# Second MLP product of a token-mixing block: five wide products per step, an order of work written by hand, low halves added to the output by transfers

## The chip, the core and the metric

The kernel runs on one core of a Trainium2 chip. The core has a matrix engine (PE, whose weight loads are listed as PEld), a vector engine (DVE), an activation engine (ACT), a general engine (POOL) and a queue engine (SP) that mostly issues transfers. They run side by side, each through its own list of instructions in order, and wait for each other by semaphores. Matrix results go to PSUM, eight banks of 2 KB per partition; everything else lies in SBUF, 128 partitions wide. Transfers between the chip's memory and SBUF run on 16 DMA engines that all queues share.

The metric is device time in microseconds (us), median over runs.

## The reference

A sequence of S = 2048 tokens of D = 512 channels goes through a linear-attention block and then through a mixer MLP, both with a residual:

```python
h  = x + _A_ref(_layernorm(x), wqkv, w_phi, wo)
# mixer: the MLP acts across the tokens, shared over the channels
hn = _layernorm(h)
u  = gelu(einsum("bsd,sf->bdf", hn, w1) + b1)      # F = 1792
y  = einsum("bdf,fs->bds", u, w2) + b2
out = h + y.transpose(0, 2, 1)
```

All data is float32, and the result must be accurate to float32's order, so a product of two matrices is made of three: each operand is split into a high part that the matrix engine takes exactly (`F32R`) and a low part (the rest), and high x high, high x low and low x high are added up.

## The kernel before, in words

The core first does the attention part, then the first MLP product (`w1`, tiles `pu`, function `fill`, helper `mm3`), then the second (`w2`, tiles `py`). The change is in the second, and in how its first weights come in while the first is still running.

**Winograd form.** The second product multiplies `w2` blocks of 2 x 2 (two blocks of 128 rows of F, two blocks of 128 output tokens) with `u` blocks of 2 x 2 (the same two blocks of F, two halves of 256 channels, `HD`). Instead of eight block products it forms seven, from sums and differences of the four blocks on each side (Strassen's scheme in Winograd's form). The `u` side, `operands_u`, makes seven operands for each pair of F blocks once and keeps their high and low parts in SBUF (`UB[p, m]`, p from 0 to 6); for p below 2 they lie in the tiles `un`, for the others in `uf`, and the last of them are made while the second product starts.

**Steps.** `STEPS` runs over 8 super-steps `sp` (two output tiles of 128 tokens each) and within each over 7 pairs `p` of F blocks: 56 steps. Each step does seven products, each of three matmuls of 128 x 128 weights and 256 columns (`product`, line 789), so 1176 matmuls. The weights are the `w2` parts, the columns the `u` parts. A super-step collects its seven products in four banks, half a bank (256 columns) for each sum that is needed; p = 0 opens them, p = 6 closes them. Odd super-steps use the banks of the pools `ps_f` and `ps_q`, even ones those of `ps_b`.

**Weights.** `stream_w2` works on groups of two steps (`GRP`): two transfers of 256 KB issued by SP (line 773, 1 KB pieces), four operations on DVE that form the sums (lines 777 to 780), ACT's copy into the high parts `whi` (line 57) and DVE's subtraction for the low parts `wlo` (line 58), 1792 elements per partition each. The raw tiles have three buffers, `whi` and `wlo` two.

**Emptying the banks.** After p = 6 the seven sums are combined: ACT copies half a bank (line 820), DVE does three additions (821 to 823) and two operations of 512 elements that add the bias `b2` (825). The two finished tiles are then added to `out`, which already holds `h`, by accumulating transfers that POOL issues (line 827). The last super-step reads `h` back into `hb` instead, adds there, and writes the sums with plain transfers (lines 830 to 847).

**Order.** Except where the code fixes it, a scheduler decides the order of each engine's instructions from a timeline of its own. In the second product it may mix the steps' matmuls, and it spreads the sums of later groups between the operations that empty banks. `issue_after(LO[-18])` keeps the first sums of `w2` behind a given low part of `w1`. SP issues the first three groups' loads of `w2` early in the first product.

The lines that matter most:

```python
def product(o, a, b, start, stop):
    for i, (x, y) in enumerate(((0, 0), (0, 1), (1, 0))):
        nc.tensor.matmul(o, a[x], b[:, y], start=start and i == 0, stop=stop and i == 2, skip_group_check=True)
```

Of the kernel before, what the change touches and what calls it, by code (L numbers as in the profile page):

```python
# [21 lines left out]
NF = F // P  # L22
NG = 8
NPR = 2 * NG
# [9 lines left out]
def block_kernel(ctx: ExitStack, tc: tile.TileContext, x, xT, wT, phic, wo, w1, b1, w2, b2,  # L34
# [20 lines left out]
    def split(hi, lo, src, lo_engine):  # L55

        nc.scalar.activation(hi, src, AF.Copy)  # L57
        lo_engine.tensor_sub(lo, src, hi)  # L58
# [535 lines left out]
    w1v = w1.rearrange("(k p) f -> p k f", p=P)  # L594
    w2v = w2.rearrange("(k p) s -> p k s", p=P)

# [7 lines left out]
    def stream(src, k0, n, c0, w):  # L604

        raw = wf.tile([P, n, w], F32, name="wraw")
        wh_ = wf.tile([P, n, w], F32R, name="whi")
        wl_ = wf.tile([P, n, w], F32R, name="wlo")
        nc.sync.dma_start(raw, src[:, k0:k0 + n, c0:c0 + w])
        nc.scalar.activation(wh_, raw, AF.Copy)  # L610
        LATER.append((wl_, raw, wh_))
        return wh_, wl_

    PU, WI, LO = {}, {}, []
    FN, FL = [0] * (NF // 2), [0] * (NF // 2)
# [93 lines left out]

    NP = NF // 2  # L710
    HD = D // 2
    up = ctx.enter_context(tc.tile_pool(name="up", bufs=1, side="right", reuse_waits="tile"))
# [50 lines left out]
    STEPS = [(sp, p) for sp in range(NT // 2) for p in range(NP)]  # L763
    GRP = 2
    AW = {}

    def stream_w2(n):
        steps = STEPS[n:n + GRP]
        raw = ws.tile([P, GRP, 7, P], F32, name="wraw", bufs=3)
        wh_ = ws.tile([P, GRP, 7, P], F32R, name="whi")  # L770
        wl_ = ws.tile([P, GRP, 7, P], F32R, name="wlo")
        for i, (sp, p) in enumerate(steps):
            nc.sync.dma_start(raw[:, i, 0:4].rearrange("p (k i) s -> p k (i s)", k=2),
                              w2v[:, 2 * p:2 * p + 2, sp * 2 * P:(sp + 1) * 2 * P])
            AW[sp, p] = wh_[:, i], wl_[:, i]
        with tc.issue_after(LO[-18]):
            nc.vector.tensor_add(raw[:, :, 4], raw[:, :, 0], raw[:, :, 2])
            nc.vector.tensor_sub(raw[:, :, 0], raw[:, :, 1], raw[:, :, 0])
            nc.vector.tensor_sub(raw[:, :, 5], raw[:, :, 4], raw[:, :, 1])
            nc.vector.tensor_sub(raw[:, :, 6], raw[:, :, 3], raw[:, :, 5])  # L780
        split(wh_, wl_, raw, nc.vector)


    PROD = ((1, 1, 0, 0, True), (2, 6, 2, 1, True), (3, 3, 3, 1, True), (4, 4, 2, 0, False), (0, 0, 1, 0, True),
            (5, 5, 0, 1, False), (6, 2, 3, 0, False))

    def product(o, a, b, start, stop):
        for i, (x, y) in enumerate(((0, 0), (0, 1), (1, 0))):
            nc.tensor.matmul(o, a[x], b[:, y], start=start and i == 0, stop=stop and i == 2, skip_group_check=True)  # L789

    def products(sp, ps, order):
        for a, b, bk, half, opens in order:
            for p in ps:
                wh_, wl_ = AW[sp, p]
                product(bank[bk][:, half], (wh_[:, a], wl_[:, a]), UB[p, b], p == 0 and opens, p == NP - 1)

    def flat(a):
        return a.rearrange("p k d -> p (k d)")

    for n, (sp, p) in enumerate(STEPS):  # L800
        t = 2 * sp
        last = t + 2 == NT
        if n % GRP == 0:
            stream_w2(n)
        if p == 0:
            pools = [ps_f, ps_f, ps_q, ps_q] if sp % 2 else [ps_b] * 4
            bank = [pool.tile([P, 2, HD], F32, name="py", tag="pu") for pool in pools]
        if p < NP - 1 - last:
            products(sp, [p], PROD)
            continue  # L810
        if p < NP - 1:
            continue
        by_bank = sorted(PROD, key=lambda m: m[2:4])
        e = uo.tile([P, 2, HD], F32, name="e")
        u2 = uo.tile([P, HD], F32, name="u2", bufs=1)
        u3 = uo.tile([P, HD], F32, name="u3")
        if not last:
            products(sp, [p], by_bank)
            ot = uo.tile([P, 2, 2, HD], F32, name="ot", bufs=1)
            nc.scalar.activation(e[:, 1], bank[0][:, 0], AF.Copy)  # L820
            nc.vector.tensor_add(u2, bank[0][:, 1], e[:, 1])
            nc.vector.tensor_add(u3, bank[1][:, 0], u2)
            nc.vector.tensor_add(e[:, 0], bank[2][:, 0], u2)
            for i, add in enumerate((u3.unsqueeze(1).to_broadcast([P, 2, HD]), e)):
                nc.vector.scalar_tensor_tensor(ot[:, i], bank[2 + i], b2s[:, t + i:t + i + 1], add,  # L825
                                               op0=ALU.add, op1=ALU.add)
                nc.gpsimd.dma_start(out[(t + i) * P:(t + i + 1) * P, :], flat(ot[:, i]), accum_op=ALU.add)  # L827
# [6 lines left out]
        products(sp, [p - 1, p], by_bank)  # L834
        nc.scalar.activation(e[:, 1], bank[0][:, 0], AF.Copy)
        nc.vector.tensor_add(hb[1][:, 1], bank[0][:, 0], hb[1][:, 1])
        nc.vector.tensor_add(u2, bank[0][:, 1], e[:, 1])
        nc.vector.tensor_add(hb[1][:, 0], u2, hb[1][:, 0])
        nc.vector.tensor_add(u3, bank[1][:, 0], u2)
        nc.vector.tensor_add(hb[0], hb[0], u3.unsqueeze(1).to_broadcast([P, 2, HD]))  # L840
        nc.vector.tensor_add(hb[0][:, 0], bank[2][:, 0], hb[0][:, 0])
        nc.vector.tensor_add(hb[1][:, 0], bank[2][:, 0], hb[1][:, 0])
        nc.vector.tensor_add(hb[0][:, 1], bank[2][:, 1], hb[0][:, 1])
        nc.sync.dma_start(out[t * P:(t + 1) * P, :], flat(hb[0]))
        for k, q in ((0, nc.scalar), (1, nc.sync)):
            nc.vector.tensor_add(hb[1][:, k], bank[3][:, k], hb[1][:, k])
            q.dma_start(out[(t + 1) * P:NT * P, k * HD:(k + 1) * HD], hb[1][:, k])


def _layout(A_x, A_wqkv, A_w_phi, A_wo, B_w1, B_b1, B_w2, B_b2):  # L850
# [7 lines left out]
    for a in range(P // DH):  # L858
        for c in range(2):
            f = (2 * c + a % 2) * DH  # L860
            mask[a * DH:(a + 1) * DH, f:f + DH] = 1.0

    wo = np.asarray(A_wo).reshape(2, 4, 2, 32, D).transpose(2, 0, 1, 3, 4).reshape(D, D)
    return {
# [6 lines left out]
        "b1": np.asarray(B_b1).reshape(NF, P).T,  # L871
        "w2": np.asarray(B_w2),
        "b2": np.asarray(B_b2).reshape(NT, P).T,
# [21 lines left out]
```

## Time and profile before

| | |
|---|---|
| median of 3 runs | 535.17 us |
| lowest and highest run | 534.43 and 535.64 us |
| span of the profiled execution, first to last instruction | 532.6 us |
| the profiled execution's own time | not recorded beside its span; the timed runs' median is 2.57 us above the span |
| PE busy | 520.8 us, 98% of the span |
| weight loads (PEld) | 448.7 us, 84% |
| DVE, ACT, POOL busy | 384.4, 271.9, 234.8 us |
| second product on PE (`py`) | 385.8 to 527.1 us |
| its matmuls | 1176, listed as 283 ns each |
| accumulating transfers | 14 of 256 KB, median 4.8 us to landing |
| loads of `w2` in 400 to 520 us | 44 of 256 KB, median 3.2 us to landing |

A matmul is listed with its full duration, but matmuls overlap: the next one starts before the last one has drained. What one costs is therefore read from start to start, not from its mean duration. The same holds, to a smaller degree, for DVE and ACT. "Idle before, releaser" names what ended an engine's waiting. The time from issue to landing of a transfer is from the queue engine's issue to the signal that the data is there.

### The profile page before, as it was taken

The page shows a single profiled execution, that of the slowest core. Times are in us where ns is not written, and L with a number is a line of the kernel's source. Part 1 is how long each engine was busy: PE and PEld are TensorE (multiplying, and loading weights), DVE is VectorE, ACT ScalarE, POOL GpSimd, SP SyncE. Part 2 cuts the span into 40 slices and gives each one's busy share as a digit, 9 for nine tenths or more (in the row PEclk, how much of TensorE's full clock was granted, in tenths as well). Part 3 has the DMA queues.
Part 4 walks back from the last instruction along what each step waited for, and adds up shares of the span by engine and source line. Part 5 has one row for each costly group of instructions (what it writes and reads, how often), then busy time and mean ns, then how long its engine had stood idle before and what let it go on. Part 6 is the DMA issues. An engine that isn't in the chain of part 4 may idle for free.

```text
span 532.6 us, 9386 instructions
## 1 busy us (share of the span) xinstructions
PE 520.8 (98%) x3616; PEld 448.7 (84%) x3616; DVE 384.4 (72%) x680; ACT 271.9 (51%) x460; POOL 234.8 (44%) x190
## 2 busy tenths in 40 slices
PE   8999999999999989999999999999999999999995
PEld 7888888886877767777788888888899999999995
DVE  6993999877699989875325524835668877887784
ACT  6998844424336776557746423525444243343340
POOL 2589699877889988887325000000001101100110
PEclk9999999999999999999999999999999999999999
DMA  8633310020502233334255333542014556535631
GB/s 309 206 110 118 99 22 21 1 72 9 160 0 79 82 101 116 104 116 136 85 176 159 98 100 98 159 117 82 20 41 107 143 148 153 123 120 136 143 75 46
DMA packets 45486, 55.81 MB, mean 105 GB/s; under 512 B 3969, under 2 KB 33025, under 8 KB 45441
## 3 DMA queue, kind: packets, MB, share of 16 engines
q1 hardware_dynamic: 43136, 51.38, 30.7%
q0 software_dynamic: 2016, 3.67, 5.5%
q8 instruction: 28, 0.46, 0.4%
q10 hardware_dynamic: 288, 0.17, 0.1%
q14 instruction: 18, 0.14, 0.1%
HBM read 46.81 MB, written 8.39 MB: 104 GB/s over the span
## 4 chain that ended last, share of the span: by engine, by line
PE 83%; POOL 9%; DVE 3%; ACT 2%; issue 1%; DVEq 0%; POOLq 0%; ACTq 0%
PE py L789 26%; PE pu L62 11%; PE pu L63 11%; PE pu L64 11%; POOL ez L442 4%; POOL eq L460 3%; PE pv L63 2%; PE pv L64 2%; PE pv L62 2%; PE pk_ps L62 2%; PE pk_ps L63 2%; PE pk_ps L64 2%; POOL hs L58 2%; PE po L62 1%; PE kvp L207 1%; PE po L63 1%
## 5 line engine op out<-in xcount | busy, mean ns | idle before, releaser
L827 POOL DMA_DIRECT2D out<-ot x14 | 12.5, 1001 | 212.2 <-DVE ot L825 212.2
L789 PE MATMUL py<-uf,whi 128*128 128x256 f32 x560 | 96.2, 283 | 0.0
L63 PE MATMUL pu<-hs,whi 128*128 128x512 f32 x224 | 87.6, 391 | 1.8 <-POOL hs L58 1.8
L602 DVE TENSOR_TENSOR wlo<-wraw,whi 128x512 fp32r<-128x512 f32 x56 | 50.3, 903 | 51.8 <-ACT whi L610 50.7
L57 ACT ACTIVATE whi<-wraw 128x1792 fp32r<-128x1792 f32 x28 | 47.7, 1705 | 77.9 <-PE py L789 73.8
L62 PE MATMUL pu<-hs,whi 128*128 128x512 f32 x224 | 87.4, 395 | 0.0
L64 PE MATMUL pu<-hs,wlo 128*128 128x512 f32 x224 | 87.2, 390 | 0.0
L789 PEld LDWEIGHTS py<-uf,whi 128*128 128x128 f32 x560 | 83.3, 192 | 0.0
L789 PE MATMUL py<-uf,wlo 128*128 128x256 f32 x280 | 69.9, 283 | 0.0
L58 DVE TENSOR_TENSOR wlo<-wraw,whi 128x1792 fp32r<-128x1792 f32 x28 | 56.6, 2022 | 15.4 <-ACT whi L57 15.4
L610 ACT ACTIVATE whi<-wraw 128x512 fp32r<-128x512 f32 x56 | 35.0, 627 | 47.0 <-PE pu L63 44.8
L63 PEld LDWEIGHTS pu<-hs,whi 128*128 128x128 f32 x224 | 42.1, 188 | 11.0 <-POOL hs L58 2.8
L62 PEld LDWEIGHTS pu<-hs,whi 128*128 128x128 f32 x224 | 42.0, 188 | 10.9 <-issue 2.5
L64 PEld LDWEIGHTS pu<-hs,wlo 128*128 128x128 f32 x224 | 42.0, 188 | 9.1 <-DVE wlo L602 0.4
L789 PEld LDWEIGHTS py<-uf,wlo 128*128 128x128 f32 x280 | 49.7, 192 | 0.0
L442 POOL TENSOR_TENSOR ez<-eq,zB 128x1024 f32<-128x1024 f32 x16 | 40.9, 2559 | 2.5 <-ACT zB L488 2.5
L789 PE MATMUL py<-un,whi 128*128 128x256 f32 x224 | 38.4, 283 | 0.0
L195 POOL TENSOR_TENSOR pk<-pk,sk 128x1024 f32<-128x1024 f32 x16 | 31.0, 1941 | 9.8 <-DVE sk L194 9.0
L460 POOL TENSOR_TENSOR eq<-eq,w 128x1024 f32<-128x1024 f32 x16 | 32.0, 1997 | 4.0 <-DVE w L457 4.0
L789 PEld LDWEIGHTS py<-un,whi 128*128 128x128 f32 x224 | 33.2, 192 | 0.1
L199 POOL TENSOR_TENSOR zacc<-zacc,pk 128x1024 f32<-128x1024 f32 x13 | 31.3, 2405 | 0.6
L58 POOL TENSOR_TENSOR hs<-hn,hs 128x512 fp32r<-128x512 f32 x16 | 21.4, 1340 | 17.5 <-ACT hs L57 15.6
(165 smaller groups left out, 1176.5 us busy)
## 6 DMA issues: line engine op xcount, KB each, us to landing
wraw<-in_w SPq DMA_DIRECT2D x112, 256.0 KB, 2.9
xraw<-in_xT SPq DMA_DIRECT2D x16, 256.0 KB, 3.1
xh<-in_x SPq DMA_DIRECT2D x16, 256.0 KB, 2.6
h<-in_x SPq DMA_DIRECT2D x16, 256.0 KB, 2.7
out<-h SPq DMA_DIRECT2D x16, 256.0 KB, 3.0
out<-ot POOLq DMA_DIRECT2D x14, 256.0 KB, 4.8
wraw<-in_wT SPq DMA_DIRECT2D x12, 256.0 KB, 5.0
wo<-in_wo SPq DMA_DIRECT2D x4, 256.0 KB, 3.6
```

Of the source, the lines that this page charges most:

```text
L57: nc.scalar.activation(hi, src, AF.Copy)
L58: lo_engine.tensor_sub(lo, src, hi)
L62: nc.tensor.matmul(o, ah, bh, start=first, stop=False)
L63: nc.tensor.matmul(o, ah, bl, start=False, stop=False)
L64: nc.tensor.matmul(o, al, bh, start=False, stop=last)
L195: nc.gpsimd.tensor_mul(heads(PK[t]), heads(PK[t]), sk.unsqueeze(2).to_broadcast([P, 2 * H, DH]))
L199: nc.gpsimd.tensor_add(zacc, zacc, PK[t])
L442: nc.gpsimd.tensor_mul(EZ[t], EQ[t], zB)
L460: nc.gpsimd.tensor_mul(heads(EQ[t]), heads(EQ[t]), W[t].rearrange("p g c h -> p (g c h)").unsqueeze(2).to_broadcast([P, 2 * H, DH]))
L602: LO.append(nc.vector.tensor_sub(wl_, raw, wh_).ins)
L610: nc.scalar.activation(wh_, raw, AF.Copy)
L789: nc.tensor.matmul(o, a[x], b[:, y], start=start and i == 0, stop=stop and i == 2, skip_group_check=True)
```

## The change

- The weight sums are chosen differently (another assignment of the same seven products, `PROD`), so that five of the seven products have a bank of their own. In these five, one matmul of 512 columns multiplies the high weights with the high and the low part of `u` side by side, into the two halves of the bank; one of 256 columns adds low weights x high `u` to the first half. The other two products share bank 2, half each, and stay three matmuls of 256 columns. A super-step has six banks instead of four, taken in turn from the eight.
- The last two pairs of every super-step (p = 5 and 6) are done together, bank by bank, so that banks are finished one after the other. Before, only the last super-step did so.
- In the last super-step one of the seven products (bank 5) stays narrow (`LAST`).
- The second half of banks 3, 4 and 5 now holds a contribution that must be added. ACT copies it into `low`, and POOL issues two more accumulating transfers per super-step (128 and 256 KB), four in all. In the last super-step DVE adds it.
- `w2` is laid out anew on the host, so that one transfer of 512 KB (4 KB in one piece for each partition) loads a group. Three operations on DVE form the sums instead of four. High parts have three buffers.
- `tc.manual_schedule` takes PE, DVE and ACT away from the scheduler for the second product; the order is the one in which the code stands: sums two groups ahead, low parts one group ahead. Where a group begins at p = 6, low parts stand between the operations that empty banks, and the sums behind them.
- `issue_after(LD[-20])` also keeps the first `w2` loads behind a given load of `w1`.
- The scratch memory for POOL's transfers is set to 8192.

```diff
+    def load_w2(g):
+        RAW[g] = ws.tile([P, 7, GRP * P], F32, name="wraw", bufs=3)
+        nc.sync.dma_start(RAW[g][:, 1:5], w2[g])
+    def sums_w2():
...
+        load_w2(g)
+        raw = RAW[g]
+        WH[g] = ws.tile([P, 7, GRP * P], F32R, name="whi", bufs=3)
+        nc.vector.tensor_add(raw[:, 0:2], raw[:, 1].unsqueeze(1).to_broadcast([P, 2, GRP * P]), raw[:, 2:4])
+        nc.vector.tensor_add(raw[:, 5], raw[:, 1], raw[:, 2])
+        nc.vector.tensor_add(raw[:, 6], raw[:, 4], raw[:, 5])
+        nc.scalar.activation(WH[g], raw, AF.Copy)
+    def lo_w2():
...
+        wl_ = ws.tile([P, 7, GRP * P], F32R, name="wlo", bufs=2)
+        nc.vector.tensor_sub(wl_, RAW[g], WH[g])
...
+    with tc.issue_after(LO[-18]), tc.issue_after(LD[-20]):
+        sums_w2()
+        lo_w2()
+        sums_w2()
+    PROD = ((2, 1, 0, None), (5, 5, 1, None), (0, 0, 2, 0), (1, 4, 2, 1), (3, 6, 3, None), (6, 2, 4, None),
+            (4, 3, 5, None))
+    LAST = PROD[:-1] + ((4, 3, 5, 0),)
+    def product(o, half, a, b, first, start, stop):
+        if half is None:
+            nc.tensor.matmul(o, a[0], b, start=start, stop=stop, skip_group_check=True)
+            nc.tensor.matmul(o[:, 0], a[1], b[:, 0], start=False, stop=stop, skip_group_check=True)
+            return
...
+    ctx.enter_context(tc.manual_schedule(engines={ET.PE, ET.DVE, ET.Activation}))
...
+        if n % GRP == 0 and p < NP - 1:
+            sums_w2()
+            lo_w2()
...
+        if p < NP - 2:
+            products(sp, [p], order)
             continue
         if p < NP - 1:
             continue
+        products(sp, [p - 1, p], order)
...
+            nc.scalar.activation(e[:, 1], bank[0][:, 0], AF.Copy)
+            for i in range(3):
+                nc.scalar.activation(low[:, i], bank[3 + i][:, 1], AF.Copy)
+            nc.vector.tensor_add(e[:, 1], bank[0][:, 1], e[:, 1])
+            nc.vector.tensor_sub(u2, bank[1][:, 0], e[:, 1])
+            nc.vector.tensor_add(u2, bank[1][:, 1], u2)
+            nc.vector.tensor_sub(u3, u2, bank[2][:, 0])
+            nc.vector.scalar_tensor_tensor(e[:, 0], bank[2][:, 1], -1.0, u2, op0=ALU.mult, op1=ALU.subtract)
...
+            out_block(0, 0, bank[2][:, 1], u3)
+            out_block(0, 1, bank[3][:, 0], u3)
+            nc.gpsimd.dma_start(out[t * P:(t + 1) * P, :], flat(ot[:, 0]), accum_op=ALU.add)
+            if n % GRP == 0:
+                lo_w2()
+            out_block(1, 0, bank[4][:, 0], e[:, 0])
+            out_block(1, 1, bank[5][:, 0], e[:, 1])
+            nc.gpsimd.dma_start(out[(t + 1) * P:(t + 2) * P, :], flat(ot[:, 1]), accum_op=ALU.add)
+            nc.gpsimd.dma_start(out[t * P:(t + 1) * P, HD:D], low[:, 0], accum_op=ALU.add)
+            nc.gpsimd.dma_start(out[(t + 1) * P:(t + 2) * P, :], flat(low[:, 1:3]), accum_op=ALU.add)
+            if n % GRP == 0:
+                sums_w2()
```

More of the change, by code (lines that the diff above doesn't have):

```diff
@@ L763, in block_kernel @@
     STEPS = [(sp, p) for sp in range(NT // 2) for p in range(NP)]
[L764 to L781, printed above, removed]
@@ L788, in product @@
+    LAST = PROD[:-1] + ((4, 3, 5, 0),)
[3 more added lines that the diff above has]
+            nc.tensor.matmul(o[:, 0], a[1], b[:, 0], start=False, stop=stop, skip_group_check=True)
+            return
         for i, (x, y) in enumerate(((0, 0), (0, 1), (1, 0))):
-            nc.tensor.matmul(o, a[x], b[:, y], start=start and i == 0, stop=stop and i == 2, skip_group_check=True)
+            nc.tensor.matmul(o[:, half], a[x], b[:, y], start=start and first and i == 0, stop=stop and i == 2,
+                             skip_group_check=True)
@@ L791, in products @@
     def products(sp, ps, order):
-        for a, b, bk, half, opens in order:
+        for a, b, bk, half in order:
             for p in ps:
                 wh_, wl_ = AW[sp, p]
-                product(bank[bk][:, half], (wh_[:, a], wl_[:, a]), UB[p, b], p == 0 and opens, p == NP - 1)
+                product(bank[bk], half, (wh_[:, a], wl_[:, a]), UB[p, b], half != 1, p == 0, p == NP - 1)
     def flat(a):
         return a.rearrange("p k d -> p (k d)")
+    ctx.enter_context(tc.manual_schedule(engines={ET.PE, ET.DVE, ET.Activation}))
@@ L802, in block_kernel @@
         last = t + 2 == NT
-        if n % GRP == 0:
-            stream_w2(n)
+        if n % GRP == 0 and p < NP - 1:
+            sums_w2()
+            lo_w2()
         if p == 0:
[L806 to L809, printed above, removed]
+            bank = []
+            for _ in range(6):
+                pool = (ps_f, ps_q, ps_b, ps_b)[n_bank % 8 // 2]
+                bank.append(pool.tile([P, 2, HD], F32, name="py", tag="pu"))
+                n_bank += 1
+        order = LAST if last else PROD
+        if p < NP - 2:
+            products(sp, [p], order)
             continue
```

70 lines of the change are left out of this document (40 added, 30 removed).

## The prediction

> **What bounds the kernel now.** I read the page first (shares, costliest groups), then the chain of waits, then windows and the timeline inside the stretch that the change touches.
>
> ```profile
> span 532.6 us, 9386 instructions
> PE 520.8 (98%) x3616; PEld 448.7 (84%) x3616; DVE 384.4 (72%) x680; ACT 271.9 (51%) x460; POOL 234.8 (44%) x190
> ```
> ```profile
> 277.65 0.91 PE pu L62 x4
> 385.99 138.25 PE py L789 x1152
> 524.26 0.39 ACT e L835
> ```
> ```profile
> 440.00:480.00 40.00, 40.00 (x335) 40.00 (x335) 33.70 (x56) 14.42 (x10) 4.80 (x6) 1.00 0.52 132
> ```
>
> The second product (tiles `py`) is one unbroken run of PE: the chain holds 1152 of its 1176 matmuls in 138.25 us, 0.1200 us each. In the window 440 to 480 us PE has no gap, DVE is busy 33.70 of 40 us, ACT 14.42, and the clock is 1.00. So a microsecond less of PE work is a microsecond less of time, as long as DVE and the loads of `w2` keep up. DVE is next in line, and it is the engine to which the change gives more.
>
> **What the change takes from PE.** The first product sets the price of a matmul of 512 columns:
>
> ```profile
> 288.82 0.39 PE L63 MATMUL pu<-hs,whi 128*128 128x512 f32 x1
> 289.50 0.39 PE L63 MATMUL pu<-hs,whi 128*128 128x512 f32 x1
> ```
>
> Three in 0.68 us, 0.2267 us each. One of 256 columns takes 0.1200, so two of them cost 0.0133 more than one wide one: every matmul carries 0.0133 us beyond its columns (512 more columns would add 0.2133). A product of three 256-column matmuls (0.360) becomes one of 512 and one of 256 (0.3467). There are 5 such products in each of 56 steps, less the 7 that the last super-step leaves narrow: 273 x 0.0133 = **-3.64 us**. A step becomes 5 x 0.3467 + 2 x 0.360 = 2.453 us instead of 2.520. No weight load limits this: PEld keeps the pace of 0.12 now, and there will be fewer loads. The rows give 0.0133 per matmul. The Trainium skill (TensorE: Matmul & The Clock Gate, Back-to-back issue gap) puts an isolated matmul at N/2.4 + 2.5 ns; by it the saving would be 0.68 us instead of 3.64, and the trace disagrees at both widths.
>
> **What it gives to DVE.**
>
> ```profile
> 399.66 0.42 DVE L777 TENSOR_TENSOR wraw<-wraw 128x256 f32<-128x256 f32 x1
> 400.11 0.42 DVE L778 TENSOR_TENSOR wraw<-wraw 128x256 f32<-128x256 f32 x1
> 400.45 0.42 DVE L779 TENSOR_TENSOR wraw<-wraw 128x256 f32<-128x256 f32 x1
> ...
> 407.03 0.74 DVE L825 SCALAR_TENSOR_TENSOR ot<-py,b2s,u 128x512 f32<-128x512 f32 x1
> 407.69 0.74 DVE L825 SCALAR_TENSOR_TENSOR ot<-py,b2s,e 128x512 f32<-128x512 f32 x1
> 408.35 2.02 DVE L58 TENSOR_TENSOR wlo<-wraw,whi 128x1792 fp32r<-128x1792 f32 x1
> 410.28 0.42 DVE L777 TENSOR_TENSOR wraw<-wraw 128x256 f32<-128x256 f32 x1
> ```
> ```profile
> 293.39 1.29 DVE L602 TENSOR_TENSOR wlo<-wraw,whi 128x512 fp32r<-128x512 f32 x2
> ```
> ```profile
> 401.02 1.70 ACT L57 ACTIVATE whi<-wraw 128x1792 fp32r<-128x1792 f32 x1 [3.34 <-PE py L789]
> ```
> ```profile
> 402.76 2.02 DVE L58 TENSOR_TENSOR wlo<-wraw,whi 128x1792 fp32r<-128x1792 f32 x1 [1.43 <-ACT whi L57]
> ```
>
> From start to start: 0.34 us for 256 elements, 0.45 where it needs the result just before, 0.60 for 512, 0.66 for a 512-element scalar form (so 0.39 for 256), 1.93 for the low parts of a group (two steps). ACT's high part takes 1.70, and DVE follows 0.04 later. A group's sums go from four operations (1.46) to three (0.60 + 0.45 + 0.45 = 1.5): nothing. Emptying the banks of a super-step (two output tiles) goes from 3 x 0.34 + 2 x 0.66 = 2.3 to nine operations of 256, 4 x 0.34 + 5 x 0.39 and three dependences of 0.11 = 3.65. Over two super-steps (14 steps, 7 groups) DVE then has 7 x 3.43 + 2 x 3.65 = 31.3 of 34.35 us, in strict order, with waits inside. ACT gets three copies of 256 per super-step (about 0.3 each): hidden, it is idle two thirds of the window. POOL issues 28 transfers instead of 14; nothing else runs there.
>
> **Where DVE comes late, even super-steps.** The written order lets one be followed by hand. T is PE's start of the merged pair of steps (5 and 6 of the first super-step, the same in every second one). The low parts of the next group may only overwrite their buffer when PE has used step 5's last ones, at T+4.56, plus 0.2 that a matmul takes to be seen by another engine:
>
> ```profile
> 384.92 0.39 PE L64 MATMUL pu<-hs,wlo 128*128 128x512 f32 x1
> ...
> 385.35 1.37 ACT L726 ACTIVATE u<-pu,b1s 128x512 f32<-128x512 f32 x2 [3.45 <-PE pu L64]
> ```
>
> (0.43 from start to start, 0.227 of it columns). So low parts T+4.8 to 6.7, two output blocks to 7.4, sums of the group after to 9.0, ACT's high part to 10.75, and behind it that group's low parts, seen by PE at T+12.85. PE wants them in its second matmul of step 10: T + 5 x 2.453 + 0.23 = T+12.5. PE waits 0.35; four even super-steps: **+1.4 us** (0.2 to 0.45 each, by how long a signal takes).
>
> **Where a load comes late.** A group's load is issued when the low parts three groups before are done, and its sums stand behind one group's sums and low parts, 3.45 us of DVE. When DVE is catching up after emptying banks, a load that needs longer holds it.
>
> ```profile
> L773 SPq DMA_DIRECT2D wraw<-in_w x2: 367/428/488, 410.4 to 410.8; - x2
> ...
> DMA to landing us min/median/max: 5.3/5.4/5.6
> ```
> ```profile
> L773 SPq DMA_DIRECT2D wraw<-in_w x2: 368/420/472, 420.0 to 420.5; - x2
> ...
> DMA to landing us min/median/max: 5.3/5.4/5.5
> ```
> ```profile
> L773 SPq DMA_DIRECT2D wraw<-in_w x2: 368/420/471, 440.1 to 440.6; - x2
> ...
> DMA to landing us min/median/max: 2.6/2.9/3.2
> ```
> ```profile
> L827 POOL DMA_DIRECT2D out<-ot x2: 863/978/1092, 423.3 to 424.0; - x2
> ...
> DMA to landing us min/median/max: 4.2/5.3/6.4
> ```
>
> A group's 512 KB land 3.6 us after the first issue where nothing adds to the output (440.1), and 5.9 beside an accumulating transfer (410.4, 420.0). Before, that cost only 1.5 us of DVE's slack. The change doubles these transfers (four per super-step, 896 KB instead of 512), two of them waiting for another's landing, so they spread from T+4.7 to about T+19.
>
> ```profile
> L773 SPq DMA_DIRECT2D wraw<-in_w x44: 367/418/575, 399.8 to 507.9; - x44
> ...
> DMA to landing us min/median/max: 2.5/3.2/6.8
> ```
>
> Odd super-steps (three), T again PE's start of the merged pair: the last bank is done at T+4.9, DVE has emptied it at T+5.9 (0.2, ACT's copy of 0.39 and one operation later), sums to 7.4, low parts to 9.4; here the critical load goes out. PE wants the low parts that stand behind its sums at T+17.75: the merged pair, five steps, and 0.58 into the next merged pair. Sums, low parts and their signals take 3.6, so the load may take 4.75. At 3.6 it costs nothing, at 5.9 it costs 1.2, and if the small transfers push it to the longest landing of this stretch, 6.8, it costs 2.05. I take 1.0, since it will always run beside accumulations and is one issue instead of two (0.4 earlier): **+3.0 us**. Even super-steps have a second such load at T+12.8, with 3.45 of cover; what it adds moves the low parts of T+9.4 in the odd super-step behind it, which PE wants at T + 4 x 2.453 + 0.23 = T+10.0, so 0.6 more is free: 0 at 3.6, 1.85 at 5.9. The accumulations are thinner by then; I take 0.3 by the 440.1 row: **+1.2 us**.
>
> **The ends.** In the tail, DVE's operations after the last banks grow from 11 to 15:
>
> ```profile
> 526.82 0.28 PE L789 MATMUL py<-uf,wlo 128*128 128x256 f32 x1
> 528.06 0.75 DVE L846 TENSOR_TENSOR hb<-py,hb 128x256 f32<-128x256 f32 x2
> ```
>
> Now DVE ends 2.0 us after PE's last start. After, it starts 1.35 into the merged pair, and thirteen operations of 0.34 with four dependences, one of 0.60 and the last one's 0.42 (5.9 in all) end at 7.2; PE's last start is at 4.85: 2.35, **+0.35** (0 to 0.8). At the start, the first three `w2` groups (1.5 MB) move fifteen places back in SP's queue and stand ahead of nineteen `w1` loads. A second 256 KB adds 1.0 us to a first (the 440.1 row: 2.6, then 0.4 + 3.2), so they hold a `w1` load back by some 6 us; `w1` has four buffers and runs three groups of 12 x 0.2267 = 2.72 us ahead, 8.2 us. ACT makes the three high parts in a row there, 5.1 us, under the same lead, and the first wide matmul, which stands in PE's order among the fifth pair's, waits for the first of them. All of it costs nothing; with the lead gone it would be about 3 us, once. PSUM: the first bank that is used again is wanted at T+5.6 and was read at about T+2, the others follow in the order in which they are emptied: nothing.
>
> **The sum.** -3.64 + 1.4 + 3.0 + 1.2 + 0.35 = +2.3 us. On the profiled execution's span of 532.6 this is 534.9; the median of the runs, 535.17, lies 2.57 above that span, so **537.5 us**.
>
> **The rivals.**
> - *The loads keep up* (faster). If every critical load lands within 3.5 to 4.7 us, the +3.0 and +1.2 vanish: -3.64 + 1.4 + 0.35 = -1.9, **533.3 us**. For it: a load becomes one piece of 4 KB per partition instead of four of 1 KB. Against it: the 420.0 row is slow although it was issued 3.3 us ahead of an accumulation. It decides at a landing of 4.75 us. The Trainium skill (DMA: Bandwidth & Descriptors, Queues, rings and completion order) says an engine turns between its queues packet by packet; by that, larger pieces would win a larger share of each turn, which would favour this rival, and no row here has such pieces.
> - *The accumulations back up* (slower still). All critical loads at 5.9 to 6.8 in both kinds of super-step: 3 x 2.05 + 4 x 1.85 = 13.55 in place of 4.2, which is +11.7, 547; with half of the even ones, **543 us**. For it: four transfers at 4.2 to 6.4 each, two of them chained, nearly fill a super-step of 17.2 us, and ACT's next copy into `low` waits for the last. Against it: half of the data goes in the gaps.
> - *The wide product saves nothing*: 535.17 + 5.9 = 541. The two pitches above speak against it; below 1 in 50.
>
> **How the numbers follow.** Loads somewhat late (536.3 to 540), 0.42; loads keep up (533 to 534.1), 0.30; back-up (540 to 547), 0.16; and 0.12 for stalls that just cancel the gain. About 0.2%, 1.07 us, is what a measurement of this kernel can tell from no change. Faster 0.30, same 0.12, slower 0.58. The range reaches down to the first rival with its stalls at 0.25 (532.9) and up to 543; the likeliest case's own is 536.3 to 540.
>
> **What would show it.** Matmuls of `py` fall from 1176 to 903 and a gapless step takes 2.45 us. PE, which had no wait in this stage, waits for DVE's low parts at the fourth step after an even merge (about 0.35 us) and at the merge after an odd one (about 1). Sums wait for the load of `w2`, DVE is over 85% busy, and loads beside accumulations land in 5 us or more. The prediction is wrong if those loads land in under 4.7 us, or if DVE's nine emptying operations overlap less with PE than the hand order says.

## The result and the profile after

The changed kernel takes 538.11 us (median of 4 runs, 537.75 to 539.4); the kernel before took 534.83 us beside it (534.43 to 535.64). The ratio is 1.0063, 95% interval 1.0047 to 1.0078: slower by 3.28 us. The profiled execution is the slowest of the four, 539.4 us, 1.8 above its span and 1.3 above the median, so what its waits add up to holds for it and not for a typical run.

The page of the changed kernel:

```profile
span 537.6 us, 8845 instructions
PE 521.9 (97%) x3343; PEld 433.8 (81%) x3343; DVE 394.8 (73%) x684; ACT 278.4 (52%) x481; POOL 247.2 (46%) x204
```

PE has 273 matmuls fewer, as counted, and is still listed as busy for longer. The chain of waits from 405 to 440 us (start, length, what) no longer stays on PE. It runs through two loads of `w2`, the sums (L782 to L784) and the low parts (L794):

```profile
411.72 6.29 DMA wraw<-in_w
418.02 0.02 issue
418.04 0.70 DVE wraw L782
...
429.20 4.85 DMA wraw<-in_w
434.07 0.70 DVE wraw L782
...
435.61 2.03 DVE wlo L794
437.64 0.04 issue
437.68 0.39 PE py L810
```

PE's timeline in that stretch, with the idle time and its releaser in brackets:

```profile
411.75 0.38 PE L810 MATMUL py<-uf,wlo 128*128 128x256 f32 x1 [0.17 <-DVE wlo L794]
...
424.55 0.51 PE L809 MATMUL py<-un,whi 128*128 128x512 f32 x1 [0.57 <-DVE ot L862]
...
429.18 0.39 PE L810 MATMUL py<-uf,wlo 128*128 128x256 f32 x1 [0.91 <-DVE wlo L794]
...
437.68 0.39 PE L810 MATMUL py<-uf,wlo 128*128 128x256 f32 x1 [0.43 <-DVE wlo L794]
```

The first kind of wait (411.75) comes back at 450.24, 486.75 and 522.88: the fourth step after each even merge. The others follow the two late loads. In the list of waits from 386 to 538 us (total, times, longest), and among the loads from 395 to 530 us:

```profile
DVE wraw L782 <- DMA wraw<-in_w: 8.8, 6, 2.9
PEld py L810 <- DVE wlo L794: 6.4, 10, 1.2
```
```profile
L771 SPq DMA_DIRECT2D wraw<-in_w x22: 327/328/328, 398.6 to 510.3; - x22
...
DMA to landing us min/median/max: 3.1/4.5/6.3
```

And the window that the prediction used:

```profile
440.00:480.00 40.00, 39.09 (x248) 34.63 (x247) 34.47 (x51) 15.92 (x18) 7.83 (x9) 1.00 0.65 143
```

PE now has gaps, DVE is busy 34.47 of 40 us (86%), and the DMA engines are busy 0.65 of the time instead of 0.52. The clock is 1.00 in both. The matmuls of a step, where nothing waits, start like this:

```profile
392.72 0.40 PE L809 MATMUL py<-uf,whi 128*128 128x512 f32 x1
392.95 0.28 PE L810 MATMUL py<-uf,wlo 128*128 128x256 f32 x1
393.07 0.40 PE L809 MATMUL py<-uf,whi 128*128 128x512 f32 x1
393.31 0.28 PE L810 MATMUL py<-uf,wlo 128*128 128x256 f32 x1
```

From 392.72 to 394.49 (the next start, not shown) five wide products take 1.77 us, 0.354 each, not 0.3467. Over the whole stage, waits left out, 0.236 us pass from the start of a wide matmul to that of the narrow one behind it, and 0.118 from there to the next wide one.

### The profile page after: what moved, and what is told of

Read it like the earlier page. It is cut to its first block, busy times and chain, and to the rows that moved or that the text cites. A ratio compares the mean times of both kernels' runs of the same rounds, so it can differ in the third digit from the quotient of the medians.

```text
span 537.6 us, 8845 instructions
## 1 busy us (share of the span) xinstructions
PE 521.9 (97%) x3343; PEld 433.8 (81%) x3343; DVE 394.8 (73%) x684; ACT 278.4 (52%) x481; POOL 247.2 (46%) x204
## 4 chain that ended last, share of the span: by engine, by line
PE 57%; DVE 15%; POOL 12%; DMA 6%; ACT 5%; issue 3%; SPq 0%; DVEq 0%; POOLq 0%; ACTq 0%
PE pu L65 10%; PE pu L66 10%; PE pu L67 10%; DMA wraw<-in_w 5%; POOL ez L445 4%; DVE wlo L794 4%; POOL eq L463 3%; PE py L809 3%; PE pv L66 2%; PE pv L67 2%; PE pv L65 2%; PE pk_ps L65 2%; PE pk_ps L66 2%; PE pk_ps L67 2%; PE py L813 2%
## 5 line engine op out<-in xcount | busy, mean ns | idle before, releaser
L866 POOL DMA_DIRECT2D out<-ot x7 | 6.2, 891 | 167.2 <-DVE ot L862 167.2
L809 PE MATMUL py<-uf,whi 128*128 128x512 f32 x195 | 71.2, 398 | 0.0
L794 DVE TENSOR_TENSOR wlo<-wraw,whi 128x1792 fp32r<-128x1792 f32 x28 | 56.4, 2021 | 4.5 <-PE py L810 2.2
L810 PE MATMUL py<-uf,wlo 128*128 128x256 f32 x195 | 55.9, 287 | 3.2 <-DVE wlo L794 3.1
L809 PEld LDWEIGHTS py<-uf,whi 128*128 128x128 f32 x195 | 36.8, 189 | 6.9
L810 PEld LDWEIGHTS py<-uf,wlo 128*128 128x128 f32 x195 | 36.9, 189 | 6.4 <-DVE wlo L794 6.4
L813 PE MATMUL py<-uf,whi 128*128 128x256 f32 x170 | 32.0, 282 | 0.0
L809 PE MATMUL py<-un,whi 128*128 128x512 f32 x78 | 29.0, 401 | 0.7 <-DVE ot L862 0.6
```

Source lines behind the costliest of these rows:

```text
L794: nc.vector.tensor_sub(wl_, RAW[g], WH[g])
L809: nc.tensor.matmul(o, a[0], b, start=start, stop=stop, skip_group_check=True)
L810: nc.tensor.matmul(o[:, 0], a[1], b[:, 0], start=False, stop=stop, skip_group_check=True)
L813: nc.tensor.matmul(o[:, half], a[x], b[:, y], start=start and first and i == 0, stop=stop and i == 2, skip_group_check=True)
```

## The experiments

Each kernel ran beside the kernel before on the same chip; that one's medians lay at 534.78 to 535.09 in all of them, so times of different groups may be compared to about 0.3 us. Where the intervals of two runs overlap, their difference is not clear of the scatter between executions.

| run | us | ratio to before, 95% interval |
|---|---|---|
| changed kernel | 538.11 | 1.0063 (1.0047 to 1.0078) |
| without the `low` transfers | 534.99 | 1.0000 (0.9992 to 1.0009) |
| narrow matmuls | 540.04 | 1.0089 (1.0074 to 1.0105) |
| high weights first | 537.59 | 1.0045 (1.0033 to 1.0058) |
| five raw buffers | 533.85 | 0.9978 (0.9964 to 0.9993) |
| pieces of 1 KB | 539.60 | 1.0100 (1.0083 to 1.0116) |
| low halves on DVE | 540.75 | 1.0114 (1.0101 to 1.0128) |
| five raw, narrow | 535.49 | 1.0013 (1.0004 to 1.0021) |
| five raw, sums and high parts early | 554.88 | 1.0375 (1.0355 to 1.0394) |
| five raw, sums early, high parts late | 532.10 | 0.9947 (0.9935 to 0.9959) |
| five raw, high weights first | 531.92 | 0.9944 (0.9932 to 0.9956) |
| order by the scheduler | 552.91 | 1.0307 (1.0269 to 1.0344) |
| five raw, high first, low halves on DVE | 535.38 | 1.0006 (0.9997 to 1.0015) |

### Are the loads late, and because of the accumulations?

```diff
-            nc.gpsimd.dma_start(out[t * P:(t + 1) * P, HD:D], low[:, 0], accum_op=ALU.add)
-            nc.gpsimd.dma_start(out[(t + 1) * P:(t + 2) * P, :], flat(low[:, 1:3]), accum_op=ALU.add)
```

> The changed kernel without its two transfers per super-step that add the low halves (14 transfers, 2.75 MB, are left out, so those contributions are missing from the output); ACT's copies into `low` stay. Theory (critical w2 loads land late because they share the DMA engines with twice the accumulations): loads of the second product land in 3.1 to 4.7 us instead of 3.1 to 6.3, the 2.89 us that the sums wait for a load at 418 us goes, and so do PE's waits at the merged pairs after odd super-steps; 2 to 4 us less than the changed kernel, 534 to 536. The 0.2 us waits at the fourth step after an even merge stay. Rival (the hand order of DVE's work alone delays PE, the loads are late only because they are waited for): no change, 538.

```diff
+    wx = ctx.enter_context(tc.tile_pool(name="wx", bufs=2, reuse_waits="tile"))
...
-        RAW[g] = ws.tile([P, 7, GRP * P], F32, name="wraw", bufs=3)
+        if g % 5 < 3:
+            RAW[g] = ws.tile([P, 7, GRP * P], F32, name="wraw", bufs=3)
+        else:
+            RAW[g] = wx.tile([P, 7, GRP * P], F32, name="wraw")
```

> The changed kernel with five raw w2 buffers instead of three (two of them in the memory that w1's tiles leave free), so that each load can be issued two groups, about 10 us, earlier. Transfers, sums and PE's order stay. Theory (late loads cost what the prediction gave them, 3.0 + 1.2 us, less what DVE's own order takes anyway): sums no longer wait for loads, although these land no faster beside accumulations; 2 to 4 us less, 534 to 536; the 0.35 us waits after even merges stay. Rival (DVE's order and the buffers of the high and low parts set the waits): 538, with sums early and PE waiting just as long.

Without the `low` transfers the time falls by 3.12 us, inside the range expected; with five buffers it falls by 4.26, to a little below it. The loads from 395 to 530 us, first without the transfers, then with five buffers:

```profile
DVE wraw L782: 2.8, 3
...
DMA to landing us min/median/max: 3.1/3.2/5.3
```
```profile
DMA to landing us min/median/max: 3.0/4.1/6.0
```

The first removes the added cause (median landing 3.2 instead of 4.5 us), the second only the harm: with five buffers loads still land in up to 6.0 us, and nobody waits for them. In both, PE's timeline keeps four waits and no others; with five buffers:

```profile
411.11 0.38 PE L814 MATMUL py<-uf,wlo 128*128 128x256 f32 x1 [0.17 <-DVE wlo L798]
...
516.96 0.39 PE L814 MATMUL py<-uf,wlo 128*128 128x256 f32 x1 [0.20 <-DVE wlo L798]
```

Both rivals (DVE's order alone makes the loss) fall. By the medians late loads cost the changed kernel 4.3 us, and about 3.1 of these come from the added transfers. The split is rough: the profiled execution without the transfers, 533.42 us, is the fastest of twelve, and in it PE loses nothing to loads any more.

### Does the size of the pieces matter?

```diff
-        nc.sync.dma_start(RAW[g][:, 1:5], w2[g])
+        nc.sync.dma_start(RAW[g][:, 1:5], w2[g].rearrange("k p s -> p k s"))
...
-    w2 = w2.reshape(-1, GRP, P, 4, P).transpose(0, 2, 3, 1, 4).reshape(-1, P, 4, GRP * P)
+    w2 = w2.reshape(-1, GRP, P, 4, P).transpose(0, 3, 2, 1, 4).reshape(-1, 4, P, GRP * P)
```

> The changed kernel with w2 laid out so that the 512 KB load of a group reads four pieces of 1 KB for each partition instead of one of 4 KB; one transfer as now, all else as now. It measures by itself what the piece size does to a load beside accumulations. Theory (a load that runs beside an accumulating transfer is late because of the bytes that the DMA engines must move, whatever the pieces): landings stay at 3.1 to 6.3 us, median 4.5, and the time at 537.5 to 538.5. Rival (larger pieces win the load a larger share of the engines, as a turn by packets would have it): landings beside accumulations grow to 5.5 to 8 us, the sums wait longer, and the time grows by 1 to 4 us, 539 to 542.

The loads of this run, from 395 to 530 us:

```profile
DMA to landing us min/median/max: 3.3/4.4/6.5
```

The landings are those of the changed kernel (3.1/4.5/6.3) to 0.2 us, as the theory has it, but the median time is 1.5 us higher, and the two intervals don't meet. The rival's time came; of its landings of 5.5 to 8 us the median shows nothing, but two of the loads that the chain of waits of this run goes through came to 5.41 and 5.68 us:

```profile
464.40 5.41 DMA wraw<-in_w
501.20 5.68 DMA wraw<-in_w
```

The same loads took 4.72 and 4.67 us in the changed kernel (465.85 and 502.02). PE waits longer behind them, 0.98 and 1.25 us instead of 0.28 and 0.24:

```profile
473.44 0.39 PE L810 MATMUL py<-uf,wlo 128*128 128x256 f32 x1 [0.98 <-DVE wlo L794]
510.51 0.39 PE L810 MATMUL py<-uf,wlo 128*128 128x256 f32 x1 [1.25 <-DVE wlo L794]
```

Other loads landed sooner here (5.93 us at 411.71, where the changed kernel's took 6.29), and the two profiled executions took the same time, 539.60 and 539.4 us. So one trace of each can't say whether the size of the pieces makes the 1.5 us between the medians or the chance of which load is late; that stays open. By the Trainium skill (DMA: Bandwidth & Descriptors, Queues, rings and completion order) an engine turns between queues packet by packet. The prediction took this to favour large pieces; the medians of the landings, 4.4 us with small pieces and 4.5 with large ones, show no such effect, and no run here shows the turns themselves.

### What are the wide matmuls worth?

In both runs the wide matmul is made in two halves:

```diff
-            nc.tensor.matmul(o, a[0], b, start=start, stop=stop, skip_group_check=True)
+            for y in range(2):
+                nc.tensor.matmul(o[:, y], a[0], b[:, y], start=start and y == 0, stop=stop and y == 1,
+                                 skip_group_check=True)
```

> The changed kernel with each wide matmul made as two of 256 columns into the same two half banks, nothing else: 273 matmuls more, 512 columns in two pieces. By the prediction's term (0.0133 us for each matmul) PE's work grows by 3.64 us; by the starts in the changed kernel's trace (0.354 for a wide product, against 0.360) by 1.6 us. If PE alone set the pace the time would be 541.7 or 539.7. Since PE also waits for low parts, and a slower PE wants them later, theory: waits take up part of it, 538.3 to 539.5, with a gapless step of 2.52 us and fewer PE waits. Rival (weights and loads set the pace of the whole stage): 538.1, unchanged, waits shrinking by all of it.

> Five raw buffers, and each wide matmul made as two of 256 columns: beside the run with five raw buffers alone it gives the worth of the wide matmuls where no load makes PE wait. By the prediction's term 273 x 0.0133 = 3.64 us more than that run, 537.5; by the starts read in the changed kernel's trace (0.354 instead of 0.360 for a product) 1.6 us more, 535.5, less up to 1.4 because a slower PE no longer meets the low parts after even merges: theory 534.0 to 535.5. Rival (wide matmuls are worth nothing here): 533.9, equal.

With three buffers 1.93 us more than the changed kernel, with five 1.64 us more. The intervals of the pair with three buffers overlap, so its excess over the 0.2 to 1.4 expected (538.3 to 539.5) is not shown; the pair with five is clear. Its 1.64 is what the starts say, 273 x (0.360 - 0.354) = 1.64, and less than half of the prediction's 3.64. The waits after even merges could have hidden more of it, as the theory allowed. They did not: the narrow run with five buffers still starts late there, although its list of waits has no line of PE, because a matmul is listed for 0.16 us beyond the start of the next one and a shorter wait does not show.

```profile
447.33 0.40 PE L814 MATMUL py<-uf,whi 128*128 128x256 f32 x2
447.84 0.39 PE L816 MATMUL py<-uf,wlo 128*128 128x256 f32 x1
448.06 0.41 PE L814 MATMUL py<-uf,whi 128*128 128x256 f32 x2
```

Two narrow matmuls should bring the third to 447.57; it starts 0.27 us later. Added up over the stage, such late starts make 1.6 us in this run and 1.85 in the run with five buffers alone, so the waits took up about 0.2. The rivals, that the wide matmuls are worth nothing, fall too, by the pair with five buffers.

### Does the order within a step matter?

```diff
+    def by_weight(sp, p, order):
+        wh_, wl_ = AW[sp, p]
+        for a, b, bk, half in sorted(order, key=lambda m: m[3] is not None):
+            high(bank[bk], half, (wh_[:, a],), UB[p, b], half != 1, p == 0)
+        for a, b, bk, half in order:
+            nc.tensor.matmul(bank[bk][:, half or 0], wl_[:, a], UB[p, b][:, 0], start=False, stop=False,
+                             skip_group_check=True)
...
-            products(sp, [p], order)
+            by_weight(sp, p, order)
```

(`high` issues the wide matmul, or the two narrow ones with the high weights.)

> The changed kernel with the matmuls of each plain step (not of the merged pairs) in another order: first all with high weights, the five wide ones in a row and then four narrow ones, then the seven with low weights. Same matmuls, same sums. Two things change: widths no longer alternate, and low parts are wanted some 1.6 us later in a step. Theory: wide matmuls in a row take 0.227 us each as in the first product (0.235 when each is followed by a narrow one), some 40 steps x 5 x 0.008 = 1.6 us less, and PE's waits at the fourth step after an even merge (about 0.35 us, four times) go too, while waits in merged pairs stay: 534.5 to 535.5. If the pitch does not depend on the neighbours: 536 to 537. If the pitch changes but DVE and loads set the pace: 538.

PE's timeline of this run, matmuls grouped by line:

```profile
395.60 1.32 PE L809 MATMUL py<-uf,whi 128*128 128x512 f32 x5
396.76 0.64 PE L812 MATMUL py<-uf,whi 128*128 128x256 f32 x4
397.23 1.00 PE L820 MATMUL py<-uf,wlo 128*128 128x256 f32 x7
398.07 0.40 PE L825 MATMUL py<-uf,whi 128*128 128x512 f32 x1
...
422.40 0.90 PE L809 MATMUL py<-un,whi 128*128 128x512 f32 x2 [1.14 <-DVE ot L878]
```

A step takes 2.47 us (395.60 to 398.07) instead of 2.49. Five wide matmuls in a row take 1.16 us (395.60 to 396.76), 0.232 each: nearer to the 0.236 of the alternating order than to the 0.2267 of the first product. But the median falls by 0.52 us only, which is not clear of the scatter, and not by the 2.6 to 3.6 expected. (The profiled execution, 535.93 us, is the fastest of six.) Five wide matmuls in a row at the head of a super-step want five banks at once, and the last row shows PE waiting 1.14 us until DVE has read one of them; this happens three times, 1.9 us in all. So the order was kept for the steps p = 1 to 4 alone, with five buffers:

```diff
-            products(sp, [p], order)
+            if p > 0:
+                by_weight(sp, p, order)
+            else:
+                products(sp, [p], order)
```

> Five raw buffers, sums where the change has them, and high weights before low weights in the steps p = 1 to 4 only (step p = 0 stays as it is, since five wide matmuls in a row there want five banks at once, which cost 0.2 to 1.1 us three times when all plain steps had this order). Theory: low parts are wanted some 1.6 us later in the fourth step after an even merge, so its 0.35 us wait goes (1.4 us), and a step takes 2.473 instead of 2.49 us, 32 x 0.017 = 0.5 us; 531.5 to 532.5, about 0.5 us below the run with early sums. Rival (something else takes the place of these waits): 533 to 534.

531.92 us, as the theory has it, and the list of waits from 386 us on has no line of PE; from start to start, too, no late one is left. This is the lowest time of all, 2.91 us below the kernel before and 6.2 below the changed one, though not clear of the run with early sums (532.10 us, in the next part).

### Where does the wait after even merges come from?

The first try moved `sums_w2()`, which also issues ACT's high part, from behind the last output blocks to ahead of the emptying:

```diff
+        if not last and n % GRP == 0:
+            sums_w2()
         e = uo.tile([P, 2, HD], F32, name="e")
...
-            if n % GRP == 0:
-                sums_w2()
```

> Five raw buffers, and in even super-steps the weight sums that stood behind the last output blocks stand ahead of the operations that empty the banks, so that ACT's high part no longer follows them late. Theory (the wait of about 0.35 us at the fourth step after an even merge comes from that chain of sums, high part, low part): the four waits at 411, 446, 482 and 517 us go, 4 x 0.35 = 1.4 us less than with five raw buffers alone, 532.4. Rival (low parts there are late because DVE has too much to do between merges, whatever the order): the waits stay or move to the merged pairs, 533.9 or up to 1 us more.

554.88 us, against 532.4. ACT's and DVE's timelines show it:

```profile
403.88 1.70 ACT L789 ACTIVATE whi<-wraw 128x1792 fp32r<-128x1792 f32 x1 [5.40 <-PE py L813]
```
```profile
405.88 0.42 DVE L861 TENSOR_TENSOR e<-py,e 128x256 f32<-128x256 f32 x1 [5.38 <-ACT e L858]
```

The high part waits until PE has left its buffer (a step of the merged pair still uses it), and ACT's copy of bank 0, issued behind it, waits along: the emptying starts over 5 us late, in each even super-step. The next run leaves the high part where it was, behind ACT's copies:

```diff
+        if not last and n % GRP == 0:
+            ahead = sums_w2(now=False)
...
                 nc.scalar.activation(low[:, i], bank[3 + i][:, 1], AF.Copy)
+            if n % GRP == 0:
+                high_w2(ahead)
```

> Five raw buffers and the sums ahead of the emptying in even super-steps as in the run before, but ACT's high part stays behind its copies of the banks, so that no copy waits behind a high part that itself waits for PE. Theory (the 554.9 came from ACT's order alone: copy of bank 0 behind a high part that waited 5.4 us for PE's use of its buffer; the sums themselves fit in DVE's idle time ahead of the emptying): the four waits of about 0.35 us after even merges go, 1.4 us less than with five raw buffers alone, 532.0 to 533.0. Rival (the sums ahead of the emptying delay the banks or the low parts by their own 1.5 us): PE waits at the first steps after an even merge or at the fourth, 533.9 to 536.

532.10 us, inside the theory's range and 1.75 below five buffers alone; no wait of PE is left, from start to start either. The sums fill what was idle time of DVE before (1.52 us ahead of the emptying at 400.08 in the changed kernel). Early sums and high weights first do the same thing to this wait, one by making low parts earlier and one by wanting them later.

### Is the written order at fault, or the choice of transfers?

```diff
-    ctx.enter_context(tc.manual_schedule(engines={ET.PE, ET.DVE, ET.Activation}))
```

> The changed kernel with the scheduler choosing the order of PE, DVE and ACT in the second product again, as in the kernel before; three raw buffers. Theory (the loss comes from critical loads, which any order with three raw buffers meets as long as the accumulations double): 537 to 540, the same waits for loads in other places. Rival (the written order, sums two groups ahead of low parts, is what makes PE wait): the scheduler moves sums and low parts between the emptying operations and PE's waits fall, 534 to 536.

```diff
-            for i in range(3):
-                nc.scalar.activation(low[:, i], bank[3 + i][:, 1], AF.Copy)
...
             out_block(0, 1, bank[3][:, 0], u3)
+            nc.vector.tensor_add(ot[:, 0, 1], bank[3][:, 1], ot[:, 0, 1])
...
             out_block(1, 1, bank[5][:, 0], e[:, 1])
+            for h in range(2):
+                nc.vector.tensor_add(ot[:, 1, h], bank[4 + h][:, 1], ot[:, 1, h])
```

(and without the two `low` transfers)

> The changed kernel with the low halves added by DVE: three more additions of 256 elements per super-step straight from the banks into `ot`, before the transfers of `ot`; ACT's three copies into `low` and the two transfers of `low` go. Same result, 14 accumulations instead of 28, about 1.3 us more of DVE in each super-step. Theory (the accumulations cost what the run without them gave, 3.1 us; DVE's extra operations stand ahead of low parts in odd super-steps and partly in even ones, and are paid only where DVE is late): between the run without the low transfers and the changed kernel, 535 to 537. Rival (DVE is so near its limit that 1.3 us in each super-step is paid in full, 7 x 1.3 = 9 less 3.1): 541 to 544.

> The best version so far (five raw buffers, high weights first in steps p = 1 to 4) with the low halves added by DVE instead of by transfers. Neither loads nor the order of low parts make PE wait in that version, so what remains is DVE's capacity: 31.3 us of written work for two super-steps, and 2 x 1.3 more, against 34.6 us of PE. Theory (DVE is now at its limit, since it also waits inside its order for PE and ACT): waits for low parts come back at the merged pairs and the time is 533 to 537. Rival (the run with low halves on DVE was slow by its order and its late loads only): no waits, 531.5 to 532.5, with half as many accumulations.

The scheduler's order is much worse than both thought, 552.91 us. Its waits from 386 to 550 us:

```profile
ACT whi L785 <- PE py L809: 44.1, 8, 7.7
ACT e L851 <- PE py L810: 30.5, 7, 4.8
DVE wraw L782 <- DMA wraw<-in_w: 28.1, 15, 3.6
```

Sums wait for loads in 15 places instead of 6. Which of its choices does the harm was not tried. So this scheduler's order is no remedy. The written order still has a part in the changed kernel's loss, the four waits after even merges, which another written order removed.

Low halves on DVE cost 2.6 us more than the changed kernel, with three buffers, although the loads then land in 3.3 us (median): PE waits 1.0 to 1.1 us after even merges instead of 0.2. That is 5.8 us above the run without the transfers, of 9 us of added DVE work: outside both ranges, nearer to the rival (541 to 544), with two thirds of the work paid, than to the theory (535 to 537). In the best order the same edit gives 535.38, 3.5 above the transfers and inside the theory's range. Its window from 440 to 480 us:

```profile
440.00:480.00 40.00, 39.53 (x252) 35.29 (x252) 37.21 (x59) 12.47 (x9) 5.00 (x6) 1.00 0.57 130
```

DVE is at 37.21 of 40 us, and waits for low parts are back at the merged pairs (435.13, 471.03, 506.95). Whether DVE has too much to do there, or only has the additions in the wrong place, ahead of low parts and sums, was not tried. So the transfers are the better place for the low halves once the loads have their buffers.

## Why the prediction was right, and where it was not

The sign and the mechanism came out, and the size came out nearer than its terms deserve: +2.3 us predicted and +3.28 measured, with two terms off that partly offset each other, and 537.5 against 538.11 because the prediction started from 535.17 and not from the 534.83 beside the changed kernel.

**What the change takes from PE: mis-sized.** The term of -3.64 us measured -1.64. The step that failed is the price of a wide matmul, 0.2267 us, carried over from the first product, where every neighbour is as wide. In the second product it is 0.236 with 0.118 behind it. Neighbours explain only a part of this: in a row it still takes 0.232, and steps come down to 2.47 us, not to the 2.453 of the sum. Why the rest is dearer than in the first product stays open. The prediction set the rows against the Trainium skill (TensorE: Matmul & The Clock Gate, Back-to-back issue gap), by which it would be 0.68 us. The measured 1.64 lies between the two.

**Even super-steps, DVE late: right.** 0.35 us each were worked out by hand. A matmul that does not wait starts 0.17 us before the listed end of the one ahead (392.95 against 392.72 + 0.40), so the four waits of 0.17 to 0.22 us lose 0.34 to 0.39 each, and the start behind each is late by another 0.1: 1.85 us in all. Removing them gave 1.75 us, against the +1.4.

**Late loads: right in sum, wrong in its split.** 3.0 + 1.2 = 4.2 us predicted, 4.26 measured with five buffers; that the sums agree is luck. The prediction gave most to the load of odd super-steps, 1.0 us each for a landing near 5.75; these loads landed in 4.67 to 4.85. By PE's waits in the profiled run, each with 0.17 added, the load of odd super-steps cost 0.60, 0.45 and 0.41 us (at 437.68, 474.19 and 510.32), and that of even ones 1.8 us in the first round (424.55 and 429.18), 0.6 in the second and 0.3 in the third (465.84, 502.01). The even load at 411.72 landed in 6.29 us, not near the 3.6 taken because "the accumulations are thinner by then": DVE had 3.45 us of cover and waited 2.89, as this row of its timeline shows.

```profile
418.04 0.69 DVE L782 TENSOR_TENSOR wraw<-wraw 128x512 f32<-128x512 f32 x1 [2.89 <-DMA wraw<-in_w]
```

Part of that loss took a way that had been priced at nothing: the next emptying came late, and PE waited 0.57 us for a bank (424.55).

**The tail: the term right, its effect not.** DVE was to end 2.35 us after PE's last start and ends 2.24 after it. Yet the span ends sooner after PE's last start, 5.02 us instead of 5.78. PE's last row and SP's last issue in the changed kernel, and SP's last issue in the kernel before:

```profile
532.58 0.28 PE L813 MATMUL py<-uf,wlo 128*128 128x256 f32 x1
```
```profile
534.85 0.34 SPq L899 DMA_DIRECT2D out<-hb  x1
```
```profile
528.84 0.36 SPq L847 DMA_DIRECT2D out<-hb  x1
```

From the last issue to the end of the span it took 3.76 us before, and 2.75 after. The three last transfers are issued 0.8 and 0.3 us apart instead of 0.3 and 0.3; that this is the reason was not tried.

**The start: right.** PE has no gap from 290 us to the end of the first product, with the three `w2` groups moved among its loads.

**The sum.** With the measured terms, -1.64 + 1.75 + 4.26 - 0.76 = +3.6 us, against +3.28 measured; 0.3 us is not accounted for. Against the predicted +2.3, PE's term is 2.0 too good, and the tail 1.1 too dear; that these two work against each other is luck.

**The rivals.** *The loads keep up* was to give 533.3 us; the run with five buffers makes that case and gives 533.85. Its bound of 4.75 us was about half a microsecond too high: the odd loads landed in 4.85, 4.72 and 4.67 us (429.20, 465.85, 502.02 in the chain), which by it costs 0.1 or nothing, and cost 0.60, 0.45 and 0.41. For the even loads the prediction's cover of 3.45 and 0.6 more fits better: landings of 6.29, 4.47 and 4.13 us would cost 2.2, 0.4 and 0.1 by it, and cost 1.8, 0.6 and 0.3. *The accumulations back up* did not happen: landings reach 6.3 us, but the median is 4.5. *The wide product saves nothing* is excluded by the narrow run with five buffers.

**What it said would show.** 903 matmuls of `py`, waits at the fourth step after an even merge, DVE over 85%, sums that wait for `w2`: all there. Waits of about 1 us at the merge after an odd super-step: there, but of 0.41 to 0.60 us. Loads of 5 us or more beside accumulations: five of 22, the others sooner. Under 4.7 us for the critical ones was to prove it wrong; with 4.67 to 4.85 the odd ones stood at that edge. A gapless step of 2.45 us: 2.49.

## What to carry to other kernels

When a stage has no gap on its bound engine, look at what each of its loads has for cover before adding transfers beside them: here a load that lands in 3.2 us without the added transfers and has 3.45 of cover was no longer covered when it took 4.5 or 6.3. More buffers for such loads (in memory that an earlier stage had left free) gave back 4.26 us, where leaving out the added transfers gave 3.12. In a hand-written order, move an instruction only after asking what its own wait blocks behind it on that engine: one high part ahead of one copy, in four super-steps, cost over 20 us. And read the price of an instruction from the stage that will use it: a matmul's price from another stage made the predicted gain more than twice too large.

## What was not expected of the hardware

- The time from one matmul's start to the next is not fixed by its columns: 512 columns took 0.2267 us in the first product, 0.232 in a row in the second, and 0.236 there ahead of one of 256. A step of five wide and eleven narrow ones takes 2.49 us alternating and 2.47 us sorted.
- Three more additions of 256 elements on DVE per super-step cost 3.5 us in all, where, with five raw buffers, ACT's copies and the accumulating transfers for the same work cost nothing that PE waits for.
- Loads of 512 KB in pieces of 1 KB and of 4 KB landed alike beside the accumulations (shortest, median and longest 3.3, 4.4, 6.5 and 3.1, 4.5, 6.3 us).
